# Attention with a relative bias, then an ELU layer pair: the ELU's steps moved a product apart, and the first block of x taken earlier

## The chip, the cores and the metric

The kernel runs on one core of a Trainium2 chip. The metric is the device time of one execution in microseconds (us), as the median of several runs. TensorE (PE) multiplies, VectorE (DVE) and ScalarE (ACT) do elementwise work, GpSimd (POOL) a little of it, and SyncE (SP) issues nearly all DMAs from one queue, in the order in which they were written. Every engine works through its own list in order, and waits where an operand isn't there yet.

## The reference, cut to what matters

The inputs are q, k, v of 4 batches x 8 heads x 576 positions x 64. Per head:

```
scores = q @ k.T / 8 + bias[head]           # bias from a small MLP of log-distances
attn   = softmax(scores)
o      = attn @ v
```

The outputs of the 8 heads of a position stand side by side, which gives x of 2304 tokens x 512. Then:

```
h   = x @ w_in                              # 512 -> 2048
g   = where(h > 0, h, exp(min(h, 0)) - 1)   # the elu
out = g @ w_out                             # 2048 -> 512
```

All of it is float32. A product of the second part is made of three passes over a high and a low part of each operand (high*high, high*low, low*high): the high part is a copy into a narrower type, the low part what is left.

## The kernel before, in words

**First part, attention.** Sixteen pairs of heads n = 0 to 15 (four batches, four pairs each), and in a pair five steps i = 0 to 4, one for each block of query rows (the third one, i = 2, is the tail of both heads). A step computes scores on PE, subtracts and takes the maximum on DVE (L303, two instructions, one in the step of the tail), takes exp on ACT (L314), copies a 64-column piece on POOL (L319), and turns the step before with transposes on PE (L355). The products with v (L399) of a pair run in the steps of the next pair, and their results go to DRAM (`xd`, L409 to L412). A list written out by hand, `STEPS`, sets the order inside a step.

Beside this, each pair takes one sixteenth of the weights (`decode`), which come in as 64-bit numbers: load (SP, L250), scale (POOL, L255), low (DVE, L259), sign (DVE, L263), shift (DVE, L265), add (POOL, L268), store to `wf` (SP, L270). The load of the next sixteenth waits for this one's sign, since they share the tile `raw`. The last pair's sixteenth is worked off partly behind the last step.

The dict `early` holds what the first block of x needs, keyed by (pair - 16, step), so (-3, 0) is pair 13, step 0. It runs at the end of that step. `load_x` brings a quarter of a block (L448) and the inverses of the softmax sums broadcast over 64 partitions (L452, tile `rr`, one buffer). A quarter of half h = 0 is 3 DMAs here, one of half h = 1 is 9, since tokens 384 to 767 lie in three stretches. `scale_x` multiplies the two on DVE (L460). `high_x` and `low_x` split the result (L483, L486). `sums_x` forms the sums T1 to T4 (L474), T1 and T3 in the place of x's own quarters, T2 and T4 in tiles that exist only in the second part. Behind the last step come the last products with v, the inversion of the sums (`invert`, L324 and L325), their transpose on PE and its copy (`turn`, L330, L332), and the splits of the first weights (`low_w`, L497).

**Second part.** Three blocks of 768 tokens (j), and for each eight groups of 256 hidden columns, so 24 products i, with j = i // 8 and q = i % 8. Products 0 and 1 (`eight`) are plain, with four steps of 12 matmuls; products 2 to 23 (`seven`) use Winograd's form of Strassen's scheme, with seven steps k of 6 matmuls (L766). After each step's matmuls, `aside(k)` issues what `plans` holds for (i, k), and `fill` issues some of the 36 matmuls (L726) of the second layer for the product before. In `seven`, k = 0, 2 share a PSUM bank, and k = 1, 3, and k = 4, 6; the sums u2, u3 and c are formed on DVE (L799).

The elu of a result is two ACT instructions (L743 relu of -h, L744 exp), one of DVE (L745), then the split: a copy on ACT (L752) and a subtraction on DVE (L753). The first three are issued in the step of the result, the last two after the matmuls of the next step.

Products 2 to 9 meet each of the eight groups of weights for the first time. `make_w(i)` forms their sums (L687 to L692) and splits (L684 on ACT, L685 on DVE) in the seven steps of product i - 1, and stores the result to DRAM (L707, L708: 1792 KB and 1024 KB a product; the two loads of raw weights, L490, are 512 KB each). From product 10 on they are fetched (L666). During products 2 to 7, and again 10 to 15, the next block of x is loaded, scaled, summed and split.

Of the kernel before, what the change touches and what calls it, by code (L numbers as in the profile page):

```python
# [15 lines left out]
ALU = mybir.AluOpType  # L16
# [8 lines left out]
def kernel(  # L25
# [484 lines left out]
    def attention():  # L510
# [15 lines left out]
        )  # L526
        late = []

        early = {
            (-4, 3): [(load_x, 0, 0, 0)],  # L530
            (-3, 0): [(scale_x, 0, 0, 0, nc.vector)],
            (-3, 1): [(load_x, 0, 0, 1)],
            (-3, 4): [(scale_x, 0, 0, 1, nc.vector)],
            (-2, 0): [(load_x, 0, 1, 0), (high_x, 0, "B11", xo["B11"], nc.vector.tensor_copy)],
            (-2, 2): [(low_x, 0, "B11", xo["B11"], nc.vector)],
            (-2, 3): [(scale_x, 0, 1, 0, nc.vector)],
            (-2, 4): [(load_x, 0, 1, 1)],
            (-1, 0): [(high_x, 0, "B12", xo["B12"], nc.vector.tensor_copy)],
            (-1, 1): [(low_x, 0, "B12", xo["B12"], nc.vector), (scale_x, 0, 1, 1, nc.vector)],
            (-1, 2): [(high_x, 0, "B21", xo["B21"], nc.vector.tensor_copy)],  # L540
            (-1, 3): [(low_x, 0, "B21", xo["B21"], nc.vector)],
        }


# [1 line left out]
        def aside(n, i):  # L546
            this, new = plan.get(n), plan.get(n + 1)
            d = lambda f, *ops: [decode(dp, f, o) for o in ops]
            if n == NP - 1:
                this = None  # L550
# [12 lines left out]

        plan = {f: f for f in range(NFC)}
        for n in range(NP):
# [4 lines left out]
            for i, u in enumerate(order):  # L570
# [39 lines left out]
                if i == 4:  # L610
                    load_w(2)
                    high_w(1)
                    decode(dp, plan.get(n), "scale")

        decode(dp, plan.get(NP - 1), "low")
        decode(dp, plan.get(NP - 1), "sign")
        decode(dp, plan.get(NP - 1), "shift")
# [4 lines left out]
        decode(dp, plan.get(NP - 1), "add")  # L622
        high_x(0, "B22", xo["B22"], nc.vector.tensor_copy)
        invert(B - 1)
        low_x(0, "B22", xo["B22"], nc.vector)
        late += pv(NP - 1, 1, (4, 0, 1, 2, 3), xp) + turn(B - 1)
        low_w(1, nc.vector)
        for fn in late:
# [6 lines left out]
    def mlp():  # L635
# [32 lines left out]
        def make_w(i):  # L668
# [21 lines left out]
            yield  # L690
            v.tensor_sub(S1[:, 1], S1[:, 0], A11)
            v.tensor_sub(S1[:, 3], A12, S1[:, 1])  # L692
            high(4)
            yield
            low(0)
            high(1)
            yield
            low(4)
            high(2)
            high(3)  # L700
            yield
            low(1)
            low(2)
            yield
            low(3)
            yield
# [30 lines left out]
                            nc.sync.dma_start(out=out[t0:t0 + P, :], in_=os)  # L737
                        yield

        def elu_a(src):  # L740

            e = ep.tile([P, HB], F32, tag="e", name="e")
            nc.scalar.activation(e, src, AF.Relu, scale=-1.0)  # L743
            nc.scalar.activation(e, e, AF.Exp, scale=-1.0)  # L744
            nc.vector.scalar_tensor_tensor(e, e, -1.0, src, op0=ALU.add, op1=ALU.max)  # L745
            return e

        def elu_b(i, e, h, x):
            if (i, e) not in g:
                g[i, e] = [gp.tile([P, 2 * HB], F32R, tag=t, name=t) for t in ("gh", "gl")]  # L750
            gh, gl = (t[:, h * HB:(h + 1) * HB] for t in g[i, e])
            nc.scalar.copy(gh, x)  # L752
            nc.vector.tensor_sub(gl, x, gh.bitcast(F32))  # L753


        def bank(k):
# [16 lines left out]
                next(rest, None)  # L773

        def eight(i, rest, aside):
            late = None
            for k, (e, h) in enumerate(((0, 0), (0, 1), (1, 0), (1, 1))):
                w = ws[2 * i + e]
                b1, b2 = (xo[f"B{r}{h + 1}"] for r in (1, 2))
# [7 lines left out]
                if late:  # L787
                    elu_b(*late)
                late = i, e, h, elu_a(ps)
                aside(k)  # L790
                fill(rest, 9)
            return late, ((0, 0), (0, 1), (1, 0), (1, 1))

        def seven(i, rest, aside, late):
            ps, u = {}, {}

            def add(name, x, y):
# [4 lines left out]
            for k, (a, b) in enumerate(PRODS):  # L802
                m = (k + i) % 2
                if k in (0, 1, 4, 5):
                    ps[k % 2] = bank(m)
                p = ps[k % 2]
                A = [[AT[i][:, f, A_AT[a], c * P:(c + 1) * P] for c in range(KH)] for f in range(2)]
                product(p, A, [[xo[b][y][:, c] for c in range(KH)] for y in range(2)], k in (0, 1, 4, 5), True)
                if late:
                    elu_b(*late)  # L810
                    late = None
                if k == 0:
                    p1 = ep.tile([P, HB], F32, tag="p1", name="p1", bufs=1)
                    nc.scalar.copy(p1, p)
                if k == 1:
                    add("u2", p, p1)
                if k == 2:
                    late = i, 0, 0, elu_a(p)
                if k == 3:
                    add("u3", p, p1)  # L820
                if k == 4:
                    late = i, 1, 1, elu_a(add("c", p, u["u3"]))
                if k == 5:
                    late = i, 1, 0, elu_a(add("c", p, u["u3"]))
                if k == 6:
                    late = i, 0, 1, elu_a(add("c", p, u["u2"]))
                aside(k)
                fill(rest, 6 if k == 6 else 5)
            return late, ((0, 0), (1, 1), (1, 0), (0, 1))


        plans = {}
# [5 lines left out]

        xo.update(zip(("T1", "T2", "T3", "T4"), slots[4:]))
        free = [slots[8], slots[1]]  # L840
        for name in ("T1", "T3", "T2", "T4"):
            sums_x(0, (name,), G)
        at(0, 0, high_w, 3)
        at(0, 1, low_w, 3, V)
        for k, name in enumerate(("T1", "T3", "T2", "T4")):
            m = (0, 3) if k == 0 else (1, k - 1)
            at(*m, high_x, 0, name, xo[name], nc.scalar.copy)
            at(*m, low_x, 0, name, xo[name], V)

        made = range(FIRST, NQ + FIRST)  # L850
        for i in made:
            q = i % NQ
            run = make_w(i)
            for e in range(2):
                at(i - 2, 1, load_w, 2 * q + e, wq if i % 2 == 0 else keep)
            for k in range(7):
                at(i - 1, k if i > FIRST else k // 2, next, run)
            at(i, 0, next, run, None)
        for i in range(NQ + FIRST, NP2):
            at(i - 2, 1, fetch_w, i, 0)  # L860
            at(i - 1, 0, fetch_w, i, 1)

        nxt = {}
        for j in range(1, NB):
            i = (j - 1) * NQ
            for n, (r, h) in enumerate(((0, 0), (0, 1), (1, 0), (1, 1))):
                at(i + 2 + n, 0, load_x, j, r, h)
                at(i + 3 + n, 0, scale_x, j, r, h, V)

        def turn_x(j, k):  # L870
            name = PRODS[k][1]
            slot = nxt[name] = free.pop()
            high_x(j, name, slot, nc.scalar.copy)
            low_x(j, name, slot, V)

        late, rest = None, iter(())
        for i in range(NP2):
            j, q = divmod(i, NQ)

            def aside(k):  # L880
                for fn, args in plans.get((i, k), ()):
                    fn(*args)
                if j + 1 < NB and q == NQ - 2:
                    if k == 1:
                        turn_x(j + 1, 0)
                    if k in (2, 3, 4, 5):
                        sums_x(j + 1, (("T1", "T3", "T2", "T4")[k - 2],), V)
                    if k == 6:
                        turn_x(j + 1, 1)
                if j + 1 < NB and q == NQ - 1:  # L890
                    free.append(xo[PRODS[k][1]])
                    if k < 5:
                        turn_x(j + 1, k + 2)

            late, order = eight(i, rest, aside) if i < FIRST else seven(i, rest, aside, late)
            for _ in rest:
                pass
            if i < FIRST:
                elu_b(*late)
                late = None  # L900
            if q == NQ - 1 and j + 1 < NB:
                xo.update(nxt)
                nxt.clear()
            if i == NP2 - 1:
                elu_b(*late)
            rest = second(i, order)
        for _ in rest:
            pass

# [65 lines left out]
```

## Time and profile before

| | |
|---|---|
| median of 3 runs | 725.71 us (724.17 to 727.44) |
| the profiled execution | 726.57 us, span 724.8 us |
| PE busy | 684.8 us (94%) |
| DVE busy | 475.0 us (66%) |
| ACT busy | 441.9 us (61%) |
| POOL busy | 81.7 us (11%) |
| first matmul of the second part | 316.56 us from the span's start |
| first matmul of product 2, of product 10 | 343.28 us, 490.32 us |

The span runs from the first instruction to the last one; 1.8 us of the execution lie outside it. Busy shares are means over stages with different limits, and PE's busy time holds waits inside of pipelined matmuls, so it is read stage by stage.

### The profile page before, as it was taken

What the parts mean: (1) busy time and instruction counts of PE and PEld (TensorE: products, weight loads), DVE (VectorE), ACT (ScalarE), POOL (GpSimd) and SP (SyncE); (2) the same over time, 40 slices, a digit from 0 to 9 for tenths busy, and PEclk for the clock granted to TensorE, in tenths of its full rate; (3) what the DMA queues carried; (4) which work ended last, traced back from release to release, by engine and by line L of the source; (5) the groups of instructions that cost most, each with busy time, mean ns of one, the idle gap of its engine ahead of it and who ended that gap; (6) DMA issues with size and microseconds to landing.
All of it is one profiled execution on the core that took longest, in us unless ns stands there. A gap on an engine that the chain in (4) does not pass through costs nothing.

```text
span 724.8 us, 13195 instructions
## 1 busy us (share of the span) xinstructions
PE 684.8 (94%) x4992; PEld 507.1 (70%) x4992; DVE 475.0 (66%) x946; ACT 441.9 (61%) x953; POOL 81.7 (11%) x106
## 2 busy tenths in 40 slices
PE   5998999999999999979999988889999999999997
PEld 3335555555555555569878867779989889898896
DVE  6995667777677769878676687654455745444443
ACT  6996777778777778737455546544444544444433
POOL 0001233222323222350000000000000000000000
PEclk9998999999999999999999999999999999999999
DMA  6997755465554588541788845668767446455302
GB/s 172 220 222 183 226 183 172 157 200 199 179 188 153 166 244 275 175 155 39 260 274 273 274 180 217 262 251 322 285 234 287 160 160 246 160 202 215 120 1 87
DMA packets 49934, 144.58 MB, mean 199 GB/s; under 512 B 13376, under 2 KB 26448, under 8 KB 42192
## 3 DMA queue, kind: packets, MB, share of 16 engines
q1 hardware_dynamic: 49136, 143.44, 59.6%
q8 instruction: 39, 0.64, 0.4%
q10 hardware_dynamic: 736, 0.31, 0.2%
q14 instruction: 23, 0.19, 0.1%
HBM read 92.14 MB, written 40.97 MB: 184 GB/s over the span
## 4 chain that ended last, share of the span: by engine, by line
PE 61%; DVE 16%; ACT 14%; DMA 4%; issue 3%; SPq 1%; POOL 0%; DVEq 0%; ACTq 0%; POOLq 0%
PE acc L726 16%; PE h L766 15%; PE ps L291 11%; PE wv L399 11%; PE wt L355 5%; ACT bo L206 3%; DVE e L745 3%; ACT e L743 2%; ACT e L744 2%; DVE gl L753 2%; DVE c L799 2%; ACT rel L183 2%; PE wm L340 1%; DVE bias L486 1%; DVE bias L685 1%
## 5 line engine op out<-in xcount | busy, mean ns | idle before, releaser
L726 PE MATMUL acc<-wB,gh 128*128 128x512 f32 x528 | 172.1, 394 | 0.0
L303 DVE CUSTOM_DVE_ANT_0 ss<-ps,bias 128x576 f32<-128x576 f32 x128 | 91.9, 755 | 61.3 <-PE ps L291 48.9
L766 PE MATMUL h<-bias 128*128 128x384 f32 x552 | 114.8, 346 | 11.7 <-DVE c L799 8.7
L314 ACT ACTIVATE ss<-ss,nm 128x576 f32<-128x576 f32 x128 | 98.2, 769 | 32.4 <-DVE nm L303 32.4
L766 PEld LDWEIGHTS h<-bias 128*128 128x128 f32 x552 | 100.6, 192 | 23.6 <-DVE c L799 8.7
L291 PE MATMUL ps<-kk,qq 64*128 64x288 f32 (+1 forms) x640 | 108.2, 422 | 2.1 <-DVE nm L303 1.8
L726 PEld LDWEIGHTS acc<-wB,gh 128*128 128x128 f32 x528 | 98.7, 189 | 14.4
L726 PE MATMUL acc<-wB,gl 128*128 128x512 f32 x264 | 104.4, 395 | 0.0
L743 ACT ACTIVATE e<-c 128x384 f32<-128x384 f32 x66 | 34.6, 525 | 110.5 <-DVE c L799 110.5
L745 DVE SCALAR_TENSOR_TENSOR e<-e,c 128x384 f32<-128x384 f32 x66 | 36.9, 559 | 75.8 <-ACT e L744 75.8
L753 DVE TENSOR_TENSOR gl<-e,gh 128x384 fp32r<-128x384 f32 x96 | 54.5, 568 | 42.4 <-ACT gh L752 42.4
L752 ACT CAST gh<-e 128x384 fp32r<-128x384 f32 x96 | 49.3, 513 | 46.3 <-DVE e L745 45.8
L291 PEld LDWEIGHTS ps<-kk,qq 64*128 64x128 f32 (+1 forms) x640 | 62.8, 178 | 20.8 <-DVE nm L303 5.4
L766 PE MATMUL h<-bias,wA 128*128 128x384 f32 x276 | 56.8, 341 | 4.3 <-DVE c L799 3.8
L766 PEld LDWEIGHTS h<-bias,wA 128*128 128x128 f32 x276 | 49.5, 188 | 10.2 <-DVE c L799 2.9
L193 PE MATMUL bps<-rel,cs 128*32 128x288 f32 x576 | 44.9, 435 | 11.3 <-ACT rel L183 7.7
L726 PEld LDWEIGHTS acc<-wB,gl 128*128 128x128 f32 x264 | 49.8, 188 | 7.8
L399 PE MATMUL wv<-pta,vv 128*64 128x320 f32 (+1 forms) x320 | 54.4, 455 | 0.2 <-ACT xs L405 0.2
L744 ACT ACTIVATE e<-e 128x384 f32<-128x384 f32 x96 | 50.5, 526 | 3.0
L355 PEld LDWEIGHTS wt<-ident,ss 64*128 64x128 f32 x1024 | 37.8, 139 | 19.6 <-issue 14.6
L399 PE MATMUL wv<-ptb,vv 128*64 128x256 f32 (+1 forms) x320 | 46.3, 394 | 2.0 <-DVE xs L405 2.0
L355 PE MATMUL wt<-ident,ss 64*128 64x64 f32 x1024 | 46.8, 230 | 0.3 <-ACT pta L379 0.3
(107 smaller groups left out, 892.1 us busy)
## 6 DMA issues: line engine op xcount, KB each, us to landing
wB<-wB SPq DMA_DIRECT2D x22, 1024.0 KB, 5.1
raw<-in_wd_dram SPq DMA_DIRECT2D x16, 1024.0 KB, 5.3
bias<-wA SPq DMA_DIRECT2D x9, 1792.0 KB
wA<-wA SPq DMA_DIRECT2D x8, 1792.0 KB, 5.7
wa<-wf SPq DMA_DIRECT2D x20, 512.0 KB, 4.6
bias<-bo SPq DMA_DIRECT2D x16, 576.0 KB, 6.4
wA<-bias SPq DMA_DIRECT2D x5, 1792.0 KB, 6.2
wf<-da SPq DMA_DIRECT2D x16, 512.0 KB, 4.5
```

What stands on the lines that cost most here:

```text
L291: nc.tensor.matmul(banks[e][:, f, 0:HS] if u < NCH else banks[0][r, f, 0:HS], lhsT=qq[r, rows], rhs=kk[r, f * HS:(f + 1) * HS], start=True ...
L303: nc.vector.tensor_tensor_reduce(out=s.rearrange("p (f x) -> p f x", f=2), in0=ps[:, :, 0:HS], in1=bap.rearrange("p (f x) -> p f x", f=2), ...
L314: nc.scalar.activation(s, s, AF.Exp, bias=nm[:, e:e + 1], scale=-1.0, accum_out=sm[:, hp, col:col + 1])
L355: nc.tensor.transpose(banks[r][:, x * TAIL:(x + 1) * TAIL], ss[q, c:c + P], ident[q, q])
L399: nc.tensor.matmul(w[e * D:(e + 1) * D, 0:N], lhsT=l, rhs=r, start=(j == first), stop=(j == end))
L726: nc.tensor.matmul(acc[j, t], lhsT=x[:, t * P:(t + 1) * P], rhs=w, start=(count[j, t] == 1), stop=(count[j, t] == 6 * NQ),)
L743: nc.scalar.activation(e, src, AF.Relu, scale=-1.0)
L744: nc.scalar.activation(e, e, AF.Exp, scale=-1.0)
L745: nc.vector.scalar_tensor_tensor(e, e, -1.0, src, op0=ALU.add, op1=ALU.max)
L752: nc.scalar.copy(gh, x)
L753: nc.vector.tensor_sub(gl, x, gh.bitcast(F32))
L766: nc.tensor.matmul(ps, lhsT=a[f][c], rhs=x[y][c], start=(start and k == 0), stop=(stop and k == len(todo) - 1), skip_group_check=not start,)
```

## The change

In the attention, the entries of `early` move up to five pairs ahead and spread over pairs 11 to 15; the quarter B22 is split there too, and T1 and T3 are summed on POOL in pairs 14 and 15. T2 and T4 are summed on DVE at the start of the second part. The last sixteenth of the weights is decoded in pair 15 like the others. 

In the second part, the elu becomes a line of three stations: relu and exp in the step of the result, L745 and the ACT copy one step later, the subtraction two steps later. `make_w` is cut into nine pieces, two of them in product i itself, and its stores go to step 3 of product i. The steps of the next block of x stand at single steps of products 2 to 7, high and low a step apart.

```
 early:
-  (-4, 3): load_x(0,0,0)             (-3, 0): scale_x(0,0,0)
-  (-3, 1): load_x(0,0,1)             (-3, 4): scale_x(0,0,1)
-  (-2, 0): load_x(0,1,0), high B11   (-2, 2): low B11    (-2, 3): scale_x(0,1,0)
-  (-2, 4): load_x(0,1,1)             (-1, 0): high B12   (-1, 1): low B12, scale_x(0,1,1)
-  (-1, 2): high B21                  (-1, 3): low B21
+  (-5, 3): load_x(0,0,0)             (-4, 1): scale_x(0,0,0)
+  (-4, 2): load_x(0,0,1)             (-4, 4): scale_x(0,0,1)
+  (-3, 0): load_x(0,1,0)             (-3, 1): high B11   (-3, 2): scale_x(0,1,0)
+  (-3, 3): load_x(0,1,1), low B11    (-2, 0): scale_x(0,1,1)
+  (-2, 1): high B12   (-2, 2): low B12
+  (-2, 3): high B21, sums T1 (POOL)  (-2, 4): low B21
+  (-1, 0): sums T3 (POOL)            (-1, 1): high B22   (-1, 2): low B22
 behind the last step:
-  decode low, sign, shift, add of the last sixteenth; high B22, low B22
 second part:
-  sums T1, T3, T2, T4 on POOL
+  at(0, 0): sums T2 on DVE      at(0, 1): sums T4 on DVE
+line = [None, None]
+def elu():
+    x, y = line
+    if y: tensor_sub(gl, t, gh)                              # DVE, result of two steps ago
+    if x: scalar_tensor_tensor(t, ...); scalar.copy(gh, t)   # DVE, ACT, of the step before
+    line[:] = None, x
+def elu_next(i, e, h, src):
+    relu(t, src); exp(t)                                     # ACT, of this step
+    line[0] = i, e, h, t, src
 seven, after the matmuls of step k:
-  elu_b(of the step before)
+  elu()
   add u2 / u3 / c
-  elu_a(this)          # relu, exp, scalar_tensor_tensor
+  elu_next(this)       # relu, exp
   aside(k); fill
 make_w: pieces in steps 0 to 6 of product i-1; now also low(1) at (i, 0), low(3) at (i, 1);
         stores at (i, 3) instead of (i, 0); load_w at (i-2, 2) instead of (i-2, 1)
 next block, o = 8 * (j - 1):
-  load at (o+2,0) (o+3,0) (o+4,0) (o+5,0), scale one product later
-  B11 at (o+6,1), sums at (o+6,2..5), T2 at (o+6,6), the other five at (o+7,0..4)
+  load at (o+2,0) (o+3,1) (o+4,0) (o+4,6), scale at (o+3,0) (o+3,6) (o+4,5) (o+5,3)
+  B11 at (o+5,2..3), sums at (o+5,5) (o+5,6) (o+6,1) (o+6,3), T2 at (o+6,5..6), the others at (o+7,0..5)
```

## Rows read from the trace of the kernel before

**Rows 1.** The page: the chain that ended last, by engine.
```profile
PE 61%; DVE 16%; ACT 14%; DMA 4%; issue 3%; SPq 1%; POOL 0%; DVEq 0%; ACTq 0%; POOLq 0%
```

**Rows 2.** Windows: stretch, length; busy of PE, PEld, DVE, ACT, POOL; clock; DMA share, GB/s.
```profile
343.28:490.32 147.04, 132.56 (x626) 113.11 (x624) 102.19 (x188) 77.48 (x149) 0.00 (x0) 0.99 0.70 248
359.55:377.02 17.47, 16.30 (x80) 13.99 (x80) 12.17 (x23) 9.32 (x19) 0.00 (x0) 1.00 0.81 271
431.56:454.12 22.56, 18.07 (x79) 15.23 (x79) 17.23 (x29) 13.60 (x25) 0.00 (x0) 0.92 0.46 175
490.32:506.07 15.75, 15.75 (x79) 14.19 (x78) 6.89 (x13) 6.61 (x14) 0.00 (x0) 1.00 0.87 313
569.09:601.54 32.45, 32.22 (x158) 28.06 (x156) 20.38 (x36) 18.42 (x35) 0.00 (x0) 1.00 0.49 194
```

**Rows 3.** Waits of PE from 316 us on: total, times, longest.
```profile
PE h L766 <- DVE c L799: 12.4, 10, 1.9
```

**Rows 4.** Timeline of DVE, 410.6 to 415.3 us (product 5): start, length; idle before, releaser.
```profile
410.69 0.55 DVE L753 TENSOR_TENSOR gl<-e,gh 128x384 fp32r<-128x384 f32 x1
411.16 0.55 DVE L799 TENSOR_TENSOR c<-h,u 128x384 f32<-128x384 f32 x1
412.86 0.56 DVE L745 SCALAR_TENSOR_TENSOR e<-e,c 128x384 f32<-128x384 f32 x1 [1.15 <-ACT e L744]
```

**Rows 5.** Timeline of ACT, 410.6 to 415.3 us.
```profile
411.74 0.53 ACT L743 ACTIVATE e<-c 128x384 f32<-128x384 f32 x1 [1.46 <-DVE c L799]
```

**Rows 6.** Timeline of SP's DMA issues, 251 to 269 us (pairs 12 and 13).
```profile
251.38 0.34 SPq L250 DMA_DIRECT2D raw<-in_wd_dram  x1
...
253.71 0.43 SPq L448 DMA_DIRECT2D xr<-xd  x1
...
262.94 0.43 SPq L448 DMA_DIRECT2D xr<-xd  x1
...
267.52 1.23 SPq L452 DMA_DIRECT2D rr<-rd  x2
```

**Rows 7.** Timeline of DVE, pairs 12 (from 241.78) and 13 (from 257.12 us).
```profile
245.28 0.76 DVE L303 CUSTOM_DVE_ANT_0 ss<-ps,bias 128x576 f32<-128x576 f32 x1 [2.06 <-PE ps L291]
...
256.07 0.69 DVE L359 COPY ptb<-wt 128x512 f32<-128x512 f32 x1
257.12 0.76 DVE L303 CUSTOM_DVE_ANT_0 ss<-ps,bias 128x576 f32<-128x576 f32 x1 [0.36 <-PE ps L291]
...
261.69 0.96 DVE L460 TENSOR_TENSOR xr<-xr,rr 128x768 f32<-128x768 f32 x1 [3.13 <-DMA rr<-rd]
262.57 0.75 DVE L303 CUSTOM_DVE_ANT_0 ss<-ps,bias 128x576 f32<-128x576 f32 x1
```

**Rows 8.** The chain that ended last, 285 to 320 us: start, us, what.
```profile
293.59 3.14 DMA rr<-rd
```

**Rows 9.** Timeline of PE, 303 to 322 us: the end of the first part.
```profile
309.56 2.53 PE L399 MATMUL wv<-ptb,vv 64*64 64x256 f32 x20 [0.95 <-DVE xs L405]
314.12 0.27 PE L330 MATMUL wr<-ident,sm 128*36 128x128 f32 x1 [2.04 <-DVE sm L325]
316.56 5.64 PE L766 MATMUL h<-bias 128*128 128x384 f32 x22 [2.17 <-DVE rs L332]
```

**Rows 10.** Timeline of DVE: the split's copy L483 at two places.
```profile
298.57 0.55 DVE L483 CAST bias<-xr 128x768 fp32r<-128x768 f32 x1
...
309.33 2.54 DVE L483 CAST bias<-xr 128x768 fp32r<-128x768 f32 x1
```

**Rows 11.** Timeline of POOL, 303 to 330 us.
```profile
309.10 2.35 POOL L268 TENSOR_TENSOR da<-da,dm 128x1024 int32<-128x1024 int32 x1 [0.81 <-DVE da L265]
311.40 2.12 POOL L474 TENSOR_TENSOR xr<-xr 128x768 f32<-128x768 f32 x1
...
323.48 1.84 POOL L474 TENSOR_TENSOR T<-xr,xr 128x768 f32<-128x768 f32 x1 [8.08 <-DMA wf<-da]
```

**Rows 12.** Window behind the first matmul of the second part (columns as in Rows 2).
```profile
318.00:320.00 2.00, 2.00 (x8) 2.00 (x7) 0.69 (x1) 0.00 (x0) 0.00 (x0) 0.50 0.60 193
```

More of the change, by code (lines that the diff above doesn't have):

```diff
@@ L527, in attention @@
         late = []
+        V, G = nc.vector, nc.gpsimd
         early = {
[L530 to L541, printed above, removed]
+            (-5, 3): [(load_x, 0, 0, 0)],
+            (-4, 1): [(scale_x, 0, 0, 0, V)],
+            (-4, 2): [(load_x, 0, 0, 1)],
+            (-4, 4): [(scale_x, 0, 0, 1, V)],
+            (-3, 0): [(load_x, 0, 1, 0)],
+            (-3, 1): [(high_x, 0, "B11", xo["B11"], V.tensor_copy)],
+            (-3, 2): [(scale_x, 0, 1, 0, V)],
+            (-3, 3): [(load_x, 0, 1, 1), (low_x, 0, "B11", xo["B11"], V)],
+            (-2, 0): [(scale_x, 0, 1, 1, V)],
+            (-2, 1): [(high_x, 0, "B12", xo["B12"], V.tensor_copy)],
+            (-2, 2): [(low_x, 0, "B12", xo["B12"], V)],
+            (-2, 3): [(high_x, 0, "B21", xo["B21"], V.tensor_copy), (sums_x, 0, ("T1",), G)],
+            (-2, 4): [(low_x, 0, "B21", xo["B21"], V)],
+            (-1, 0): [(sums_x, 0, ("T3",), G)],
+            (-1, 1): [(high_x, 0, "B22", xo["B22"], V.tensor_copy)],
+            (-1, 2): [(low_x, 0, "B22", xo["B22"], V)],
         }
@@ L612, in attention @@
                     high_w(1)
[L613 to L617, printed above, removed]
         late += pv(NP - 1, 0, (0, 1, 2, 3, 4), xp)
@@ L621, in attention @@
             pass
-        decode(dp, plan.get(NP - 1), "add")
-        high_x(0, "B22", xo["B22"], nc.vector.tensor_copy)
         invert(B - 1)
-        low_x(0, "B22", xo["B22"], nc.vector)
         late += pv(NP - 1, 1, (4, 0, 1, 2, 3), xp) + turn(B - 1)
@@ L692, in make_w @@
             v.tensor_sub(S1[:, 3], A12, S1[:, 1])
+            low(0)
+            yield
             high(4)
-            yield
-            low(0)
-            high(1)
             yield
@@ L699, in make_w @@
             high(2)
+            yield
+            low(2)
+            high(1)
+            yield
             high(3)
@@ L702, in make_w @@
             low(1)
-            low(2)
             yield
@@ L738, in second, with elu @@
                         yield
[L740 to L753, printed above, removed]
+        line = [None, None]
+        def elu(tile=None):
+            x, y = line
+            if y:
+                i, e, h, t = y
+                gh, gl = (w[:, h * HB:(h + 1) * HB] for w in g[i, e])
+                nc.vector.tensor_sub(gl, t, gh.bitcast(F32))
+            if x:
+                i, e, h, t, src = x
+                if (i, e) not in g:
+                    g[i, e] = [gp.tile([P, 2 * HB], F32R, tag=w, name=w) for w in ("gh", "gl")]
+                nc.vector.scalar_tensor_tensor(t, t, -1.0, src, op0=ALU.add, op1=ALU.max)
+                nc.scalar.copy(g[i, e][0][:, h * HB:(h + 1) * HB], t)
+            line[:] = None, x and x[:4]
+        def elu_next(i, e, h, src):
+            t = ep.tile([P, HB], F32, tag="e", name="e")
+            nc.scalar.activation(t, src, AF.Relu, scale=-1.0)
+            nc.scalar.activation(t, t, AF.Exp, scale=-1.0)
+            line[0] = i, e, h, t, src
         def bank(k):
@@ L786, in eight, with seven @@
                 )
-                if late:
-                    elu_b(*late)
-                late = i, e, h, elu_a(ps)
+                elu()
+                elu_next(i, e, h, ps)
                 aside(k)
                 fill(rest, 9)
-            return late, ((0, 0), (0, 1), (1, 0), (1, 1))
-        def seven(i, rest, aside, late):
+            return (0, 0), (0, 1), (1, 0), (1, 1)
+        def seven(i, rest, aside):
             ps, u = {}, {}
@@ L814, in seven @@
                     nc.scalar.copy(p1, p)
+                elu()
                 if k == 1:
@@ L817, in seven @@
                 if k == 2:
-                    late = i, 0, 0, elu_a(p)
+                    elu_next(i, 0, 0, p)
                 if k == 3:
@@ L821, in seven @@
                 if k == 4:
-                    late = i, 1, 1, elu_a(add("c", p, u["u3"]))
+                    elu_next(i, 1, 1, add("c", p, u["u3"]))
                 if k == 5:
-                    late = i, 1, 0, elu_a(add("c", p, u["u3"]))
+                    elu_next(i, 1, 0, add("c", p, u["u3"]))
                 if k == 6:
-                    late = i, 0, 1, elu_a(add("c", p, u["u2"]))
+                    elu_next(i, 0, 1, add("c", p, u["u2"]))
                 aside(k)
                 fill(rest, 6 if k == 6 else 5)
-            return late, ((0, 0), (1, 1), (1, 0), (0, 1))
+            return (0, 0), (1, 1), (1, 0), (0, 1)
         plans = {}
@@ L840, in mlp @@
         free = [slots[8], slots[1]]
[L841 to L851, printed above, removed]
+        at(0, 0, sums_x, 0, ("T2",), V)
+        at(0, 1, sums_x, 0, ("T4",), V)
+        at(0, 1, high_w, 3)
+        at(0, 2, low_w, 3, V)
+        for (m, k), name in (((0, 2), "T2"), ((0, 3), "T3"), ((1, 1), "T1"), ((1, 2), "T4")):
+            at(m, k, high_x, 0, name, xo[name], nc.scalar.copy)
+            at(m + (k + 1) // 4, (k + 1) % 4, low_x, 0, name, xo[name], V)
+        for i in range(FIRST, NQ + FIRST):
             q = i % NQ
@@ L854, in mlp @@
             for e in range(2):
[L855 to L858, printed above, removed]
+                at(i - 2, 0 if i - 2 < FIRST else 2, load_w, 2 * q + e, wq if i % 2 == 0 else keep)
+            for k in (0, 1, 1, 2, 2, 3, 3) if i == FIRST else (0, 1, 2, 3, 4, 5, 6):
+                at(i - 1, k, next, run)
+            at(i, 0, next, run)
+            at(i, 1, next, run)
+            at(i, 3, next, run, None)
         for i in range(NQ + FIRST, NP2):
@@ L863, in mlp, with turn_x @@
         nxt = {}
-        for j in range(1, NB):
[L865 to L876, printed above, removed]
+        def turn_x(j, n, part):
+            name = PRODS[n][1]
+            if part == 0:
+                nxt[name] = free.pop()
+                high_x(j, name, nxt[name], nc.scalar.copy)
+            else:
+                low_x(j, name, nxt[name], V)
+        for j in range(1, NB):
+            o = (j - 1) * NQ
+            for (r, h), l, m in (
+                ((0, 0), (2, 0), (3, 0)), ((0, 1), (3, 1), (3, 6)), ((1, 0), (4, 0), (4, 5)), ((1, 1), (4, 6), (5, 3)),
+            ):
+                at(o + l[0], l[1], load_x, j, r, h)
+                at(o + m[0], m[1], scale_x, j, r, h, V)
+            at(o + 5, 2, turn_x, j, 0, 0)
+            at(o + 5, 3, turn_x, j, 0, 1)
+            for name, m in (("T1", (5, 5)), ("T3", (5, 6)), ("T2", (6, 1)), ("T4", (6, 3))):
+                at(o + m[0], m[1], sums_x, j, (name,), V)
+            at(o + 6, 5, turn_x, j, 1, 0)
+            at(o + 6, 6, turn_x, j, 1, 1)
+            for k in range(5):
+                at(o + 7, k, turn_x, j, k + 2, 0)
+                at(o + 7, k + 1, turn_x, j, k + 2, 1)
+        rest = iter(())
         for i in range(NP2):
@@ L880, in aside @@
             def aside(k):
+                if q == NQ - 1:
+                    free.append(xo[PRODS[k][1]])
                 for fn, args in plans.get((i, k), ()):
                     fn(*args)
[L883 to L895, printed above, removed]
+            order = (eight if i < FIRST else seven)(i, rest, aside)
             for _ in rest:
                 pass
[L898 to L901, printed above, removed]
+            if q == NQ - 1:
                 xo.update(nxt)
                 nxt.clear()
-            if i == NP2 - 1:
-                elu_b(*late)
             rest = second(i, order)
+        elu()
+        elu()
         for _ in rest:
```

6 lines of the change are left out of this document (removed).

## The prediction

> **What bounds the kernel now.** The page's chain of waits gives PE 61%, DVE and ACT 30% together [rows 1]: most of the time PE sets the pace, and somewhere the two elementwise engines do. The timeline of PE, cut at the first matmul of each product, says where. From product 10 on a product takes 15.75 us and PE is busy in all of it. Products 2 to 9, in which weights are made, take 147.04 us instead of 8 x 15.75 = 126.0, so 21.0 us are lost there; product 3 takes 17.47, product 7, where the next block of x is split too, 22.56. Products 15 and 16 lose 32.45 - 31.5 = 0.95 [rows 2]. The waits of PE name the cause: 12.4 us for the sums c of DVE, in 10 waits [rows 3], since the sum must be read before its PSUM bank is written again.
>
> The timelines of DVE and ACT in product 5 show why c is late although DVE is busy only 12.17 us of a product such as 3 [rows 2]. c starts at 411.16; ACT's relu can't start before 411.74, having idled 1.46 us for it [rows 5]; then comes exp, and DVE waits 1.15 us in front of L745 until 412.86 [rows 4]. DVE works in order, so the splits of weights behind L745 and the next c wait as well. With three such elus at steps 4, 5, 6, about 3.5 us of DVE's time is dead in a product, and ACT waits in turn.
>
> Two smaller losses lie in the first part. In pair 13 DVE waits 3.13 us at `scale_x` for the first quarter's `rr` [rows 7]. Behind the last pair PE waits 0.95 + 2.04 + 2.17 = 5.16 us [rows 9], because DVE's split of B22 and the inversion stand beside POOL's add and sums: L483 takes 2.54 us there and 0.55 elsewhere [rows 10], while POOL runs 2.35 and 2.12 [rows 11].
>
> **The change part by part.** The sum is made against the profiled execution, 726.57 us, which is 0.86 above the median of 725.71.
>
> *The elu as a line, and the weights' pieces.* No instruction is added; L745 and the copy go one step later, the subtraction two. A step is 15.75 / 7 = 2.25 us long. L745 then finds exp done: from the start of c to L745 it was 412.86 - 411.16 = 1.70 us [rows 4], less than a step. So DVE's 1.15 us in front of each L745 go, and what is left is whether DVE's work fits. Product 7 is the fullest: 4 x 2 of the elu, 5 sums c and u, 4 sums and 5 low parts of weights, 5 low parts of x, 27 instructions. Its row has 17.23 us for 29, so 0.594 each and 16.0 for 27; where they stand one behind another, starts are 0.47 apart at a length of 0.55 [rows 4], 0.08 less, which makes 13.9 at the least. Against 15.75 it just fits. Products 5 and 6 are near it, the others have over 2 us to spare. PE isn't held by a lag below 2.7 us: from the end of a step's matmuls to the reuse of its bank lie two steps less the 6 matmuls of one, some 3.4 us, of which c takes 0.55. I leave 1.5 of the 21.0 us (0 if the lag always stays under that, 8 if products 5 to 8 keep half of what they lose now), a gain of 19.5, and take the 0.95 of products 15 and 16 in full: -20.4.
>
> The last product's tail keeps its length: its 27 matmuls of the second layer ahead of the last quarter cover the two calls of `elu()` behind it.
>
> *T2 and T4 on DVE at the start of the second part.* They were POOL's, and the first waited 8.08 us, until 323.48, for the store of the last sixteenth of the weights [rows 11]. That store is still issued behind the third and fourth load of weights, so DVE now waits at T2 until about 7 us after the first matmul, with the elu's L745 behind it. The first steps use separate banks; the first bank is used again after four steps of 12 matmuls, some 10 us in. Two sums at 0.95 and one elu fit before that: 0, between -1 and +2.
>
> *The earlier first block of x.* Moving `load_x` moves 3 or 9 DMAs of SP. The second quarter's nine now stand in pair 12, step 2, behind the load of `raw`, about where the first quarter's stood: 253.7 us [rows 6]. Nine took 262.94 to 268.75 [rows 6], 5.8 us; the last starts at 258.9, and a last `rr` took 3.14 us to land [rows 8]: 262.0. DVE comes to this quarter's `scale_x` behind the copy that ends at 256.76 [rows 7], two steps later, and waits 5.3 us. With its 0.88 the next L303 starts at 262.9 instead of 257.12, 5.8 late. PE, which has two score banks, stands behind it. The wait that goes from pair 13 was worth 3.13 + 0.88 - 2.06 = 1.95, 2.06 being DVE's usual idle there [rows 7]. Net +3.8: -2 if the DMAs land in time, +7 if they take as long as the first quarter's, which needed some 3 us more behind `raw`.
>
> The fourth quarter's nine come in pair 13, step 3: `raw` went out 9.6 us into pair 12 [rows 6, 7], some 0.7 of that for the inversion, which pair 13 hasn't; two stores and the load of v follow (1.8), so the nine start at 10.7 and land at 10.7 + 5.2 + 3.1 = 19.0. A pair is some 15.2 us (pair 12: 241.78 to 257.12), so DVE is there at 16.7, behind two L303 of the next one, and step 1's L303, 3.50 us into it, is due at 18.7 but starts at 19.9: +1.2 (0 to 3). The loads of the first and third quarter have ten us and are hidden.
>
> A PE that stood for some 4 us came back at half clock: behind the waits at 312 to 316 us the granted clock is 0.50 [rows 12]. The wait in pair 12 is as long; a few us at half rate cost 0 to 1.7, I take +1.0.
>
> T1 and T3 go beside DVE's splits in pairs 14 and 15. L483 beside POOL shows what that may cost: up to 2.12 us each [rows 10, 11], 0 to 4.2; both pairs have some 2 us of DVE slack and most DVE work there reads PSUM, so I take +0.5. The Trainium skill (SBUF — State Buffer, Who interferes with whom) speaks against this edit: GpSimd and VectorE share a pair of ports under an exclusive lock, and the loser blocks for the whole instruction. The rows agree, 2.54 against 0.55; taken in full it would put the sum 3.7 us higher.
>
> *The end of the first part.* POOL's sums and B22's split leave it, and `invert` isn't held any longer; POOL's add (2.35) now ends before the last products with v do. Of PE's 5.16 us of waits the copy L332 of the sums (0.28) and its hops stay: -4.8 (-2 to -6). The last sixteenth's decode adds 2.6 us to pair 15's DVE, in which two scales' worth of other work is gone: 0.
>
> *Sum.* First part: 3.8 + 1.2 + 1.0 + 0.5 - 4.8 = +1.7. Second: -20.4. 726.57 - 18.7 = 707.9, and 707 against the median.
>
> **The rivals.**
>
> *DVE or DMA is full in products 2 to 8.* By full lengths product 7 has 16.0 us of DVE for 15.75, 5 and 6 about as much; and a product moves 2 x 512 + 1792 + 1024 KB = 3.93 MB, which at the 271 GB/s of product 3 takes 14.5 us, its share being 0.81 already [rows 2]. For: little slack on two resources. Against: 313 GB/s at 0.87 in product 10. If 5 us more stay: 713.
>
> *The loads in pairs 12 and 13 land in time.* If the queue runs ahead of what I worked out, 3.8, 1.2 and 1.0 go and 1.95 is won: 707 - 8 = 699. Against it: `raw` must wait for sign, and nine issues take 5.8 us whatever else.
>
> *The change doesn't do what it says.* The in-order wait returns in another place: the copy on ACT now waits for L745, relu for c, and the subtraction on DVE for the copy. If each step goes round both engines once, half of the gain is lost: 717. Against: within a step each of these was made ready a step before.
>
> *Slower: the next block's x parks DVE.* The `rr` of each quarter is issued when the scale before it is done, and stands behind a product's 3.93 MB of weights in the queue. Scales are now 6, 6 and 5 steps apart, 13.6, 13.6 and 11.3 us, where they were seven. If the bytes ahead move at 202 GB/s or so, 19.4 us and 3.1 to land, each scale stops DVE, and PE behind it, by 8.9, 8.9 and 11.2 us, 29 in all: 736. It comes out slower than before once three rounds exceed 38.5 + 19 us, thus under 245 GB/s. For: product 7 shows 175 GB/s [rows 2]. Against: less was asked for there (share 0.46), and stages that ask for more got 271 to 313.
>
> **How the numbers follow.** The forecast has 0.60 and its own range is 702 to 713; DVE or DMA full 0.15 (713); in time 0.12 (699); half the gain 0.06 (717); slower 0.05 (736), and 0.02 for a gain as large as the loss in the first part, which would be no change. About 0.5%, 3.6 us, is what a measurement of this kernel can tell from no change. Faster: 0.60 + 0.15 + 0.12 + 0.06 = 0.93; same 0.02; slower 0.05. The range that leaves out 2 in 10 is 699 to 717.
>
> **What would show it.** The elu: products 2 to 9 at 15.75 to 16 us each, no idle DVE in front of L745, and PE's waits for c near zero. The first block: DVE idle some 5 us at a `scale_x` in front of pair 13, and PE with it; 2 us more in pair 14. The end of the first part: PE without a wait of over 0.5 us between the last products with v and the first matmul of the second part. The prediction is wrong if DVE stops at L460 in products 3 to 5, or if PE waits in product 7 as long as now.

## The result and the profile after

The changed kernel takes 708.5 us (median of 4 runs, 706.2 to 710.13) beside 725.36 us of the kernel before on the same chip: a ratio of 0.976, 95% interval 0.973 to 0.980. Forecast were 707, between 699 and 717. The profiled execution took 708.4 us, its span is 706.6.

The page after (busy time, and the chain that ended last; answers to [rows 1]):
```profile
PE 679.3 (96%) x4992; PEld 508.7 (72%) x4992; DVE 470.7 (67%) x948; ACT 440.6 (62%) x953; POOL 75.3 (11%) x104
...
PE 51%; issue 1%; DVE 1%; ACT 1%; DMA 0%; SPq 0%; ACTq 0%
```
The chain is followed back to 316 us only, the end of the first part, which is why its shares add up to little over half. From 337 us (in product 1) to 700 it is PE's but for one wait of 0.95 us. Ahead of that, in products 0 and 1, it runs through the splits of DVE and ACT and through a stop of DVE at T2 (read off the chain in order of time):
```profile
321.59 5.15 issue
```
DVE and ACT are about as busy as before.

Windows after, cut at PE's first matmuls: products 0 and 1, products 2 to 9, product 3, product 7 (columns as in [rows 2]):
```profile
319.47:346.86 27.39, 26.07 (x132) 23.22 (x133) 17.59 (x28) 15.80 (x30) 0.00 (x0) 1.00 0.47 148
346.86:473.12 126.26, 126.26 (x625) 113.52 (x625) 103.95 (x190) 79.66 (x154) 0.00 (x0) 1.00 0.80 289
362.68:378.43 15.75, 15.75 (x79) 14.20 (x78) 12.53 (x23) 9.38 (x19) 0.00 (x0) 1.00 0.74 268
425.69:441.61 15.92, 15.92 (x79) 14.10 (x78) 15.08 (x27) 12.32 (x22) 0.00 (x0) 1.00 0.74 261
```
Products 2 to 9 take 126.26 us, 8 x 15.78, where they took 147.04; product 7 takes 15.92 with DVE busy in 15.08 of it. All the waits of PE over 0.15 us in the second part, with none for c (answers to [rows 3]; L772 is now the product):
```profile
PE h L772 <- issue: 0.9, 1, 0.9
PE h L772 <- DVE rs L332: 0.5, 1, 0.5
PE h L772 <- DVE e L751: 0.4, 2, 0.2
```
Timeline of DVE in product 4 (answers to [rows 4]; L751 is now the step after exp): three elus in 4.8 us, in which DVE idles in front of the last only, 0.48 us, and L803 (c) comes right behind the first two. The elu's stations lie a step of a product apart, some 2.25 us, and not a product, as the title has it.
```profile
390.26 0.56 DVE L751 SCALAR_TENSOR_TENSOR e<-e,c 128x384 f32<-128x384 f32 x1
390.77 0.56 DVE L803 TENSOR_TENSOR c<-h,u 128x384 f32<-128x384 f32 x1
...
392.92 0.55 DVE L751 SCALAR_TENSOR_TENSOR e<-e,c 128x384 f32<-128x384 f32 x1
393.39 0.55 DVE L803 TENSOR_TENSOR c<-h,u 128x384 f32<-128x384 f32 x1
...
395.09 0.56 DVE L751 SCALAR_TENSOR_TENSOR e<-e,c 128x384 f32<-128x384 f32 x1 [0.48 <-ACT e L758]
```
DVE's waits for exp didn't go altogether. First the kernel before from 343 to 491 us, then the changed one from 310 to 480 (total, times, longest); 6.0 of the 9.7 us lie in products 2 to 9, and no wait of PE there comes from them:
```profile
DVE e L745 <- ACT e L744: 31.7, 29, 2.0
DVE e L751 <- ACT e L758: 9.7, 14, 2.7
```
The first part has the two new stops. DVE at the scales of the second and the fourth quarter, the latter in pair 14 (answers to [rows 7]):
```profile
255.28 0.69 DVE L359 COPY ptb<-wt 128x512 f32<-128x512 f32 x1
261.09 0.96 DVE L460 TENSOR_TENSOR xr<-xr,rr 128x768 f32<-128x768 f32 x1 [5.12 <-DMA rr<-rd]
261.97 0.75 DVE L303 CUSTOM_DVE_ANT_0 ss<-ps,bias 128x576 f32<-128x576 f32 x1
...
284.51 0.96 DVE L460 TENSOR_TENSOR xr<-xr,rr 128x768 f32<-128x768 f32 x1 [4.08 <-DMA xd<-xs]
```
PE behind the first of them, and at the end of the first part (answers to [rows 9]):
```profile
262.78 2.96 PE L291 MATMUL ps<-kk,qq 64*128 64x288 f32 x8 [3.89 <-DVE nm L303]
...
316.84 1.95 PE L399 MATMUL wv<-ptb,vv 128*64 128x256 f32 x16 [0.58 <-ACT ptb L359]
318.71 0.28 PE L330 MATMUL wr<-ident,sm 128*36 128x128 f32 x1
319.47 4.42 PE L772 MATMUL h<-bias 128*128 128x384 f32 x24 [0.47 <-DVE rs L332]
```
and the clock behind the first stop, a window of TensorE's row (answers to [rows 12]):
```profile
262.00:268.00 6.00, 5.22 (x16) 2.58 (x17) 3.46 (x10) 4.48 (x11) 0.53 (x3) 0.50 0.83 223
```

Cut at the first L303 of a pair, pairs 12, 13, 14 and the rest up to the second part took 15.34, 17.46, 14.94 and 27.04 us before, 21.60, 17.02, 18.71 and 21.77 after: 4.3 us more in all. The second part from product 2 to PE's last matmul took 376.9 and takes 355.1, 21.7 less; products 0 and 1 take 0.7 more. The remaining 1.4 lie ahead of pair 11, where both kernels have the same code: in the nine profiles pair 11 begins between 224.3 and 227.1 us. These 1.4 us are luck of the two profiled executions and no gain of the change. A granted clock of 0.50 for 6.83 us, from 68.3 us on, in the profile before and not in the changed kernel's, fits them.

### The profile page after: what moved, and what is told of

Its sections match the earlier page's. It is cut to its first block, busy times and chain, and to the rows that moved or that the text cites. A ratio compares the mean times of both kernels' runs of the same rounds, so it can differ in the third digit from the quotient of the medians.

```text
span 706.6 us, 13181 instructions
## 1 busy us (share of the span) xinstructions
PE 679.3 (96%) x4992; PEld 508.7 (72%) x4992; DVE 470.7 (67%) x948; ACT 440.6 (62%) x953; POOL 75.3 (11%) x104
## 4 chain that ended last, share of the span: by engine, by line
PE 51%; issue 1%; DVE 1%; ACT 1%; DMA 0%; SPq 0%; ACTq 0%
PE acc L723 27%; PE h L772 24%; DVE bias L497 0%; DMA out_dram<-os 0%; DVE e L751 0%; ACT e L758 0%; ACT gh L752 0%; DVE xs L486 0%; ACT bias L493 0%; DVE gl L746 0%; ACT e L757 0%; ACT xs L483 0%; DVE os L732 0%; DMA wf<-da 0%; ACT os L732 0%
## 5 line engine op out<-in xcount | busy, mean ns | idle before, releaser
L303 DVE CUSTOM_DVE_ANT_0 ss<-ps,bias 128x576 f32<-128x576 f32 x128 | 91.8, 754 | 58.9 <-PE ps L291 50.2
L291 PE MATMUL ps<-kk,qq 64*128 64x288 f32 (+1 forms) x640 | 110.2, 423 | 7.9 <-DVE nm L303 7.6
L772 PE MATMUL h<-bias 128*128 128x384 f32 x552 | 111.8, 339 | 0.8 <-DVE rs L332 0.5
L772 PEld LDWEIGHTS h<-bias 128*128 128x128 f32 x552 | 99.6, 188 | 9.0 <-DVE e L751 1.9
L752 ACT CAST gh<-e 128x384 fp32r<-128x384 f32 x96 | 49.4, 514 | 44.8 <-DVE e L751 44.2
L746 DVE TENSOR_TENSOR gl<-e,gh 128x384 fp32r<-128x384 f32 x96 | 53.2, 554 | 18.1 <-ACT gh L752 15.8
L772 PE MATMUL h<-bias,wA 128*128 128x384 f32 x276 | 56.3, 338 | 0.9 <-issue 0.9
L751 DVE SCALAR_TENSOR_TENSOR e<-e,c 128x384 f32<-128x384 f32 x66 | 36.7, 557 | 30.1 <-ACT e L758 29.9
L757 ACT ACTIVATE e<-h 128x384 f32<-128x384 f32 x28 | 13.8, 491 | 68.3 <-PE h L772 68.3
L193 PE MATMUL bps<-rel,cs 128*32 128x288 f32 x576 | 45.5, 430 | 10.7 <-ACT rel L183 7.8
L772 PEld LDWEIGHTS h<-bias,wA 128*128 128x128 f32 x276 | 50.1, 188 | 5.0 <-issue 1.4
L803 DVE TENSOR_TENSOR c<-h,u 128x384 f32<-128x384 f32 x66 | 36.7, 556 | 20.1 <-PE h L772 20.1
## 6 DMA issues: line engine op xcount, KB each, us to landing
wA<-bias SPq DMA_DIRECT2D x5, 1792.0 KB, 10.7
```

The costliest lines, as they stand in the source:

```text
L193: nc.tensor.matmul(ps[32 * g:32 * g + 32, f, 0:HS], lhsT=W2, rhs=rel[g][:, f * HS:(f + 1) * HS], start=True, stop=True,)
L291: nc.tensor.matmul(banks[e][:, f, 0:HS] if u < NCH else banks[0][r, f, 0:HS], lhsT=qq[r, rows], rhs=kk[r, f * HS:(f + 1) * HS], start=True ...
L303: nc.vector.tensor_tensor_reduce(out=s.rearrange("p (f x) -> p f x", f=2), in0=ps[:, :, 0:HS], in1=bap.rearrange("p (f x) -> p f x", f=2), ...
L746: nc.vector.tensor_sub(gl, t, gh.bitcast(F32))
L752: nc.scalar.copy(g[i, e][0][:, h * HB:(h + 1) * HB], t)
L757: nc.scalar.activation(t, src, AF.Relu, scale=-1.0)
```

## The experiments

Each kernel's time stands beside runs of the kernel before on the same chip: 726.48 us for `line_only`, `line_undone`, `first_as_before` and `scales_later`, 726.77 for the other three. The edits are shortened, and partly put in words. Line numbers differ from kernel to kernel, so each group of lines says what they are.

**The elu's line alone** (`line_only`), on the kernel before:
```
-late = i, e, h, elu_a(ps)      # and elu_b(*late) a step later
+elu()                          # subtraction of two steps ago; scalar_tensor_tensor and copy of the last
+elu_next(i, e, h, ps)          # relu, exp
```


> The kernel before, with the elu's line of three stations alone; the weights' pieces, the next block's x and the first part stay as before. Theory (DVE's in-order wait in front of L745 is what made c late): products 2 to 5 take 15.75 to 16 us, PE's waits for c fall from 12.4 us to under 4; products 6 and 7, where high and low of x still stand in one step, keep 2 to 4 us; 706 to 710 in all, the first part unchanged. Rival (the cutting up of the weights and of x gives the gain): products 3 to 5 stay above 17 us, 720 or more.

Measured: 717.86 us, 0.988 (0.985 to 0.992). Windows of product 2, 3 and 7:
```profile
348.14:365.51 17.37, 17.37 (x79) 15.64 (x80) 11.93 (x24) 9.85 (x20) 0.00 (x0) 0.90 0.86 287
365.51:381.26 15.75, 15.75 (x80) 14.19 (x78) 12.32 (x25) 9.06 (x19) 0.00 (x0) 1.00 0.86 301
428.51:450.95 22.44, 17.82 (x79) 15.34 (x78) 15.64 (x27) 12.88 (x23) 0.00 (x0) 0.92 0.44 166
```
The mechanism holds where it was read: products 3 to 6 take 15.75 each. The time was missed, at two places. Product 7 keeps all it lost, 22.44, and products 0 and 1 take 33.7 us instead of 26.7. At each of the two PE's waits are followed by a granted clock of 0.50 for 3.4 us. That is all that product 2 loses (PE is busy in the whole of its 17.37 us), and some 1.7 us of what product 7 loses, here as in the kernel before (clock 0.92 over its window). Two lines of DVE's timeline in product 1 of this run, and PE's wait for the `scalar_tensor_tensor` (L752; L773 is the product) from 312 to 350 us, say how:
```profile
333.71 0.96 DVE L486 TENSOR_TENSOR xs<-xr,xs 128x768 fp32r<-128x768 f32 x1 [2.25 <-ACT xs L483]
...
338.53 0.96 DVE L486 TENSOR_TENSOR bias<-T,bias 128x768 fp32r<-128x768 f32 x1 [2.25 <-ACT bias L483]
```
```profile
PE h L773 <- DVE e L752: 4.6, 2, 3.5
```
`high` (ACT, L483) and `low` (DVE, L486) of x stand in one step here. ACT comes to the copy only behind relu and exp of the step's own result, and DVE stands at the subtraction meanwhile. The `scalar_tensor_tensor` of that result now comes a step later, behind the subtraction, and PE waits for it, since it frees the bank. One in-order wait was taken out and another of the same kind, 2.25 us a time, came to light. The changed kernel has `low` a step behind `high` in products 0 and 1 as well (T2 at (0, 2), T3 at (0, 3), T1 at (1, 1), T4 at (1, 2)), which the list of the change leaves out.

**The line undone** (`line_undone`), on the changed kernel:
```
 def elu_next(i, e, h, src):
     relu; exp
+    nc.vector.scalar_tensor_tensor(t, t, -1.0, src, ...)
 def elu():
+    copy and subtraction of the last step
-    subtraction of two steps ago; scalar_tensor_tensor and copy of the last
```


> The changed kernel with the elu as it was before: relu, exp and the scalar_tensor_tensor in the step of the result, copy and subtraction in the next. All else as changed. Theory: products 2 to 5 go back to about 17.4 us, 6 and 7 to 18 to 20, DVE idles 1.15 us in front of each of three elus again: 722 to 728. Rival (pieces and x give the gain): under 714.

Measured: 716.91 us, 0.988 (0.985 to 0.990), products 2 to 9 in 137.5 us (16.2 to 17.0 in products 3 to 5, 19.7 in product 7). Waits of DVE and of PE in them (L756 is the step after exp, L755 exp, L770 the product, L801 the sums):
```profile
DVE e L756 <- ACT e L755: 28.7, 25, 1.5
...
PE h L770 <- DVE c L801: 7.5, 9, 1.4
```
The waits for exp and for c are back, 28.7 and 7.5 us, so the sign of the theory holds. The time is neither the theory's nor the rival's: the price is 11.2 us of the 20.8, and the other 9.6 are what the moved pieces of x and of the weights are worth without the line. The rival is half right.

**x as before** (`x_as_before`): high and low of the next block's x in one step each; its loads, scales and sums go back to their old steps too. The line and the pieces are as changed.
```
-at(o+5, 2) high B11, at(o+5, 3) low B11; sums at (5,5) (5,6) (6,1) (6,3); T2 at (6,5), (6,6); ...
+q == 6: k == 1 high and low B11; k in 2..5 one sum each; k == 6 high and low T2
+q == 7: k in 0..4 high and low of the other five
```


> The changed kernel with the next block's x at the steps of the kernel before (blocks 1 and 2), the elu's line and the weights' pieces as changed. Theory (with high on ACT and low on DVE in one step, DVE waits in order for ACT, as in the run of the line alone, where product 7 took 22.44): products 6 and 7 lose 1 to 2 and 4 to 6.5 us, all others stay at 15.75: 714 to 717. Rival (DVE's load is what counts, and it is the same): under 711.

Measured: 713.6 us, 0.982 (0.979 to 0.984), 0.4 under the expected range; products 2 to 9 take 132.3 us, 6.0 more than in the changed kernel. Products 6 and 7, and two lines of DVE's waits around them:
```profile
408.33:424.26 15.93, 15.93 (x80) 14.10 (x79) 14.93 (x27) 9.16 (x18) 0.00 (x0) 1.00 0.72 277
424.26:445.97 21.71, 17.77 (x80) 15.20 (x79) 15.72 (x28) 12.12 (x22) 0.00 (x0) 0.92 0.51 185
```
```profile
DVE bias L486 <- ACT bias L483: 4.2, 3, 2.4
...
DVE xs L486 <- ACT xs L483: 1.8, 1, 1.8
```
DVE is busy 15.72 us in a product of 21.71, against 15.08 of 15.92 in the changed kernel: not its load but the order holds it, and the rival falls. In the changed kernel the waits for ACT's copy are 0.2 us in products 2 to 9, and no scale waits in either place. Only product 7 is hit; I had given product 6 a share as well.

**The weights' pieces as before** (`pieces_as_before`): make_w in seven pieces, all in product i - 1, stores at step 0.
```
-[S1, S3, low 0] [high 4] [low 4, high 2] [low 2, high 1] [high 3] | (i,0) [low 1], (i,1) [low 3], (i,3) stores
+[S1, S3, high 4] [low 0, high 1] [low 4, high 2, high 3] [low 1, low 2] [low 3] | (i,0) stores
```


> The changed kernel with make_w in the seven pieces of the kernel before, its stores at step 0 of the next product; the elu's line and x as changed. Theory (with the line, products 3 to 5 were at 15.75 even with these pieces): products 3 to 5 at 15.75, 6 and 7 lose 0 to 2, product 2 and the two before it lose 1 to 4 since there the pieces stand two to a step: 709 to 713. Rival (the pieces carry part of the gain of their own): products 3 to 5 above 16.2, 715 or more.

Measured: 707.63 us, 0.973 (0.970 to 0.975), products 2 to 9 in 126.05 us, none over 15.8. With the line and x moved, the new pieces are worth nothing that can be seen; I had expected 1 to 4 us.

**The first part as before** (`first_as_before`): old `early`, the last sixteenth and B22 behind the last step, T1 and T3 on POOL at the start of the second part, all else as changed.
```
-(-5, 3) ... (-1, 2)  the new early
+(-4, 3) ... (-1, 3)  the old one; decode low, sign, shift, add and B22 behind the last step
+for name in ("T1", "T3"): sums_x(0, (name,), G)
```


> The changed second part behind the first part of the kernel before (its early entries, the last sixteenth decoded behind the last step, B22 split there, T1 and T3 summed on POOL at the start of the second part). Theory (the two halves of the change are separate, and the earlier x costs in the first part what pairs 12 to 15 show, 57.33 us for pairs 12 to 14 against 47.74, less 5.3 won behind pair 15): the second part starts 4 us earlier, 704 to 705. Rival (the earlier x is needed for the second part, which else starts with DVE behind): products 0 to 2 give the 4 us back, 708 or more.

Measured: 705.05 us (701.87 to 706.71), 0.970 (0.968 to 0.973); products 2 to 9 in 126.3 us. So the earlier x isn't what makes the second part fast, and as it was placed it costs about what its pairs show: the whole first-part half of the change is a loss. The profile of this run has pair 11 and the first matmul of the second part at 227.1 and 317.6 us, 90.5 apart, the changed one at 225.2 and 319.5, 94.3 apart. The slowest run here and the fastest of the changed kernel overlap, so the loss rests on these windows as well as on the times.

**The scales later** (`scales_later`), on the changed kernel:
```
-(-4, 4): scale_x(0,0,1)   (-3, 0): load_x(0,1,0)   (-3, 1): high B11   (-3, 2): scale_x(0,1,0)
-(-3, 3): load_x(0,1,1), low B11   (-2, 0): scale_x(0,1,1)   (-2, 3): high B21, sums T1
+(-3, 0): high B11   (-3, 1): scale_x(0,0,1), load_x(0,1,0)   (-3, 3): low B11
+(-3, 4): scale_x(0,1,0), load_x(0,1,1)   (-2, 0): high B21   (-2, 3): scale_x(0,1,1), sums T1
```


> The changed kernel with the entries of the first block's x at other steps: the second quarter is scaled one step and a half later (pair 13, step 1), the third loaded behind that and scaled in pair 13, step 4, the fourth loaded there and scaled in pair 14, step 3; B21's high part moves to pair 14, step 0. Same instructions. Theory (DVE parks at a scale whose DMAs are still on the way, and the clock falls behind that): pairs 12, 13 and 14 take 15.2 to 15.6 us each, no half clock, 57.3 - 46.2 = 11 us less: 697 to 699. Rival (DVE is full in these pairs, or POOL's sums hold it): they stay above 16.5 us each, 704 or more.

Measured: 697.76 us (697.4 to 697.81), 0.961 (0.959 to 0.963), as expected in all, but not pair by pair. Pairs 12 to 14:
```profile
239.50:255.45 15.95, 15.95 (x160) 9.13 (x159) 12.51 (x28) 11.93 (x34) 4.34 (x6) 1.00 0.65 195
255.45:271.81 16.36, 16.36 (x164) 9.52 (x164) 15.35 (x29) 12.45 (x33) 5.23 (x7) 1.00 0.81 238
271.81:287.21 15.40, 15.40 (x158) 8.77 (x156) 15.40 (x30) 11.81 (x32) 6.70 (x8) 1.00 0.73 212
```
47.7 us instead of 57.3, the clock at full rate throughout. The same instructions, the loads of the second to fourth quarter given a step or two more before they are needed. Pairs 12 and 13, at 15.95 and 16.36, were expected at 15.6 at most. In pair 13 DVE is near full, and two of its instructions are long beside POOL: a split's copy, 1.78 us where it takes 0.55 alone [rows 10], beside POOL's add of the weights (255.81 to 258.17), and the scale of a quarter, 1.68 us instead of 0.96, beside POOL's scale of the weights (261.89 to 263.01):
```profile
256.81 1.78 DVE L483 CAST bias<-xr 128x768 fp32r<-128x768 f32 x1
...
262.14 1.68 DVE L460 TENSOR_TENSOR xr<-xr,rr 128x768 f32<-128x768 f32 x1
```

**The store first** (`store_first`), on top of `scales_later`:
```
+decode(dp, plan.get(NP - 1), "store")
 invert(B - 1)
 ...
 load_w(3); high_w(2); low_w(2)
-decode(dp, plan.get(NP - 1), "store")
```


> scales_later with one more move: the store of the last sixteenth of the weights is issued before the inversion and the last stores of x, not behind the fourth load of weights. Theory (products 0 and 1 are 2.3 us longer in the changed kernel than with the elu undone, 27.40 against 25.14, because DVE stops at T2 for this store with the elu of the first product behind it): DVE's idle of 5.2 us in front of T2 falls under 1, products 0 and 1 take 25.0 to 25.4 us, 695.3 to 696.3 in all. Rival (the elu's later steps themselves cost this in products 0 and 1): 27 us, 697.5 to 698.

Measured: 696.4 us (695.3 to 696.52), 0.958 (0.956 to 0.959), 0.1 above the expected range. First the changed kernel's DVE at T2, then this one's:
```profile
326.74 0.96 DVE L474 TENSOR_TENSOR T<-xr,xr 128x768 f32<-128x768 f32 x1 [5.15 <-issue]
327.61 0.55 DVE L751 SCALAR_TENSOR_TENSOR e<-e,h 128x384 f32<-128x384 f32 x1
```
```profile
311.95 0.94 DVE L474 TENSOR_TENSOR T<-xr,xr 128x768 f32<-128x768 f32 x1
313.39 0.56 DVE L750 SCALAR_TENSOR_TENSOR e<-e,h 128x384 f32<-128x384 f32 x1 [0.50 <-ACT e L757]
```
The 5.15 us are gone and products 0 and 1 take 25.11 us, where `scales_later`, with a stop of 4.78 us, took 27.03. It takes the stop at T2 and the line together: `line_undone` has the stop and takes 25.14, since its `scalar_tensor_tensor` stands ahead of T2. The intervals of the two ratios overlap, so the gain of 1.4 us rests on the windows more than on the times. This is the fastest version found, about 30 us under the kernel before and 12 under the changed one.

## Why the prediction was right, point by point

*The sum.* The first part was forecast at +1.7 and came to +4.3; the second at -20.4, and came to -21.7 + 0.7 = -21.0; and 1.4 us of the difference of the two profiles are luck. So the medians lie 16.9 us apart where 18.7 were forecast. The forecast held because the second part carries it; the first part's loss was put at under half of what it was.

*The second part.* Forecast -20.4; products 2 to 9 gave 20.8, products 15 and 16 the full 0.95, so -21.7. The 1.5 us that I left were too many: DVE's 15.08 us of product 7 lie between the 13.9 and 16.0 of the bounds, and PE has no wait for c. (The bound on the lag should read 3.4 - 0.55 = 2.9 us, not 2.7; nothing hangs on it.) DVE's idle time in front of L745 fell from 31.7 us to 6.0 in products 2 to 9 and not to nothing, as I had put it. The cause I named, this idle time, carries a little over half. The line alone gave 12.7 of the 20.8 us in products 2 to 9, and taking it out of the changed kernel cost 11.2. Some 6 us more come from x: with its two halves in one step, product 7 is at 21.71 even with the line. I had read product 7's 22.56 us as more of the same wait. DVE did wait 3.4 us for exp there, but 1.9 for ACT's copy of x as well, and that wait seemed small, and grew to 6.8 us once the other was gone. First the kernel before, 343 to 491 us, then `line_only`, 424 to 450:
```profile
DVE bias L486 <- ACT bias L483: 1.9, 1, 1.9
```
```profile
DVE bias L486 <- ACT bias L483: 6.0, 4, 1.8
DVE xs L486 <- ACT xs L483: 0.8, 1, 0.8
```
So this part of the sum was right by the sum of its edits and only partly by the cause given.

*T2 and T4 on DVE.* Forecast 0, with -1 to +2: products 0 and 1 take 0.7 us more. The step that failed is "two sums at 0.95 and one elu fit before that": they come 5.15 us late with every later split behind them, not only one elu, and cost 1.9 to 2.3 (`store_first` against `scales_later`, `line_undone` against the changed kernel). At the first bank, where I had looked, PE waited 0.16 us only; product 1 takes 18.65 us where it took 16.72. Most of it was hidden by something that I hadn't counted: PE no longer idles in front of the second part, so its first 3.4 us at half clock [rows 12] are gone, and product 0 takes 8.75 us where it took 9.99.

*The loads.* The stop in pair 12 was forecast at 5.3 us and was 5.12, by the three rows it was made of. The clock fell to 0.50 as it had behind the idle time at 312 us, but stayed there for 6.83 us and not 3.4: pair 13 took 17.02 us, and `scales_later`, without the stop, 16.36. Pairs 12 and 13 together cost 5.8 us more than before, forecast were 4.8. The fourth quarter's stop was forecast at 2.3 us and was 4.08, pair 14 at +1.2 and +0.5 and was +3.8: the nine DMAs started 12.9 us into pair 13, not 10.7, and took 7.1 us to issue rather than 5.8, while DVE came to the scale 18.5 us in, not 16.7. The slow clock fits the two late starts: DVE waited 1.71 us for PE's transposes in front of the copy L359, ahead of pair 13's sign, and `raw` and the nine stand behind that sign. The two late starts, of some 2 us each, nearly cancel in this wait, so what made it longer is mainly the nine's issue; why they took 7.1 us was not tried. The step that failed is the one that took pair 13 at its usual 15.2 us and the nine at their usual 5.8.

*POOL's sums* show next to no cost in pairs 14 and 15: no split of DVE there met T1 (1.83 us) or T3 (1.85); B22's copy met POOL's scale of the weights behind T3 and took 1.17 us. No run left the sums out, so their share isn't measured. What `scales_later` paid beside POOL's other work shows that this was a matter of place. By the rule of the Trainium skill that the prediction weighed (SBUF — State Buffer, Who interferes with whom), a split that meets an instruction of POOL waits for its end. The 1.78 us there against 0.55 agree, the copy having ended 0.4 us behind POOL's add; the full 3.7 us that the rule would have put on this sum didn't come, since nothing met.

*The end of the first part.* Forecast -4.8; PE's waits there fell from 5.16 us to 0.58 + 0.47 = 1.05, and pair 15 with its tail took 5.3 us less. The 0.58 is just over the 0.5 that I had named as the sign.

*The rivals.* No L460 of the second part has a wait, so the next block's x didn't park DVE; DMA carried 289 GB/s at a share of 0.80 through products 2 to 9. DVE was not full. The loads were not in time, and what they would have given, 699, is about what `scales_later` got (697.76) by giving them time. That the in-order wait returns in another place is what the line alone shows; it came back at the split of x, not at the hand-overs of the elu that this rival named, and the changed kernel had moved that split too.

## What to carry to other kernels

Where two engines pass a result back and forth, put one step of other work between each pair of hand-overs, and do it for all such pairs at once: the line alone left PE waiting for the next pair of the same kind. An operation moved earlier takes its DMAs with it: count the issues ahead of them in the queue (0.6 us each here), and place the consumer by that. A free-looking instruction at the head of an in-order engine is dear when it waits for a buffer, whatever it costs itself.

## What the runs showed of the hardware that I had not expected

The same kind of idle time gave two lengths of half clock. At the end of the old first part, behind some 4.2 us of PE's waits, the clock was at 0.5 for 3.41 us in the kernel before and in `line_only`, and for 6.83 us in `first_as_before`, whose code there is the same; behind the stop of 3.89 us in pair 12 it was 6.83 us, and eight score matmuls took 2.96 us there that take 1.19 at full clock. Near 68 us, in code that all nine kernels share, PE waits 1.1 to 2.3 us for DVE ahead of score matmuls; behind that the clock is at 0.50 for 6.83 us in two of the nine profiles, for 3.41 in two, and not at all in five. The length of the wait doesn't sort them: 1.31 us stand ahead of one of the 6.83, 2.10 ahead of one that kept the full clock. What decides was not tried. A copy and a two-input operation of DVE took 1.78 and 1.68 us beside POOL's work in `scales_later`, 0.55 and 0.96 elsewhere, while the score operation, which reads PSUM and one SBUF operand, kept its 0.75 us beside POOL's sums.
